# One unit's two 32-row inverse halves merged an iteration after their substitution, with a compact state worked in 64x64 tiles

## The chip, the cores and the metric

The kernel runs on one core of a Trainium2 chip. The metric is the device time of one execution in microseconds. TensorE is called PE here, VectorE DVE, ScalarE ACT, GpSimd POOL, and SyncE SP. All arithmetic is in 32-bit floats.

## The reference

A recurrence over 768 tokens (4 batches, 8 heads, head dimension 40), followed by a mixture of four small networks:

```python
for t in range(S):
    y[:, :, t] = np.einsum('bhd,bhde->bhe', rt, state)
    Sa = np.einsum('bhde,bhe->bhd', state, at)
    state = state * wt[:, :, None, :] - np.einsum('bhd,bhe->bhde', Sa, bt) \
          + np.einsum('bhd,bhe->bhde', vt, kt)
...
p = domain_probs / (domain_probs.sum(-1, keepdims=True) + 1e-09)
for e in range(E):                      # 4 networks, 320 -> 1024 -> 320
    h = np.maximum(x @ w1[e], 0.0)
    out += p[:, e:e + 1] * (h @ w2[e])
```

Here x is y with the heads side by side: 3072 tokens of 320 values.

## The kernel before

The tokens are cut into 12 chunks of 64. A *unit* is one chunk of two batches, so its 128 partitions hold 2 x 64 tokens; there are 24 units, numbered u = 0 to 23, two to a chunk (an even unit holds batches 0 and 1, an odd one batches 2 and 3). Inside a unit the recurrence is turned into matrix products, and these need the inverse of a unit triangular 64x64 matrix for each batch and head.

`within(u)` (L239) does what does not need the state. It transposes the decays (`pw`), forms their running product G with a scan (L247), transposes it back (`pg`), scales the inputs by G or 1/G (A, K, N; L256 to L264), transposes those (RT, VT, AT, NT, KT) and forms the products `pf`. DVE copies the 32x32 diagonal blocks of `pf` into `Fd` (L283, eight copies) and transposes them into X (L292). POOL then inverts all those blocks at once by substitution on X, with 60 dependent instructions (L296 and L300): **the substitution**. Beside it PE forms `pc`, `pyc`, `pe` and `pev`. Then comes **the merge**: DVE transposes X into QTc and Qc (L319, L320), POOL copies the diagonal blocks into QT (L331), PE forms `pY` and `pQ` from the 32-row halves (L336, L347), and ACT copies the off-diagonal block into QT (L352).

`step(u, xT)` (L358) does what needs the state, one link after another: `prh` from the state and AT, RH = prh + EV on DVE (L374), `prt` (RH transposed), `psa` from RHt and QT (the first use of the merged inverse), SaT, `pst`, `px`, the masked copy of `px` into TT on DVE (L236), the state's update (`psd` on PE, L411 and L412 on DVE), `py`, Y = py * G (L433), Y + YC on POOL (L434), and twelve small DMAs of Y into xT (L443).

`mixture(c)` (L449) runs the four networks on a finished chunk, in 32 *pieces* of PE work (`ph`, 6 matmuls, and `po`, 4 matmuls). The driver (L528) goes through the units: it writes step(u), then within(u + 2), and behind each `yield` one or two pieces of the mixture of the chunk before.

A scheduler fixes each engine's order when the kernel is built. It follows the order in which the code is written, but moves an instruction ahead where it counts the engine as free and the operands as ready. On the chip each engine runs its list in that order, and an instruction that waits holds up all that stand behind it on its engine. In the order before, POOL has: substitution u + 1, QT copies of u + 1, Y of u, substitution u + 2.

Of the kernel before, what the change touches and what calls it, by code (L numbers as in the profile page):

```python
# [15 lines left out]
def kernel(  # L16
# [12 lines left out]
):  # L29

# [90 lines left out]
    w_shift = kept("w_shift", [P, 2 * NJ, L], 1)  # L121
# [7 lines left out]
    state = [kept(f"state{i}_", [P, NJ, 2, 64], 1)() for i in range(B)]  # L129
# [7 lines left out]
    def load(u):  # L137
# [4 lines left out]
        for x in srcs:  # L142
            if x in nat:
                t = nat[x]()
            else:
                t = sb.tile([P, H, D], FP32, name=f"nat{x}", tag=f"nat{x}")
            q.n[x] = t
            for i, bb in enumerate(q.b):
                nc.sync.dma_start(
                    out=t[i * L:(i + 1) * L, :, 0:D],  # L150
                    in_=srcs[x][bb, :, q.c * L:(q.c + 1) * L, :].rearrange("h t e -> t h e"),
                )
# [41 lines left out]

    def heads(x):
        return x.rearrange("p (h e) -> p h e", e=64)
# [25 lines left out]
    def from_tokens(name, x, m):  # L222

        p = big(name)
        for j in range(NJ):
            for s in range(2):
                h = 2 * j + s
                nc.tensor.matmul(  # L228
                    out=p[half(s), j * P:(j + 1) * P], lhsT=x[:, h, :], rhs=m[:, h, :], start=True, stop=True,
# [3 lines left out]
    def causal(p):  # L233
        m = TT()
        for s in range(2):
            nc.vector.copy_predicated(out=of_slot(m[:], s), mask=over_heads(mask_up), data=p[s])  # L236
        return m

    def within(q):  # L239
# [7 lines left out]
        nc.vector.tensor_tensor_scan(  # L247
            out=q.G[:].rearrange("p c i -> p (c i)"), data0=ws[:].rearrange("p c i -> p (c i)"),
# [9 lines left out]
        nc.vector.tensor_tensor(out=A[:, :, 0:D], in0=pg, in1=n["A"][:], op=ALU.mult)  # L258
# [8 lines left out]
        def turned(name, x, keep=False):  # L267
            t = sb.tile([P, NJ, P], FP32, name=name, tag=name if keep else "turned", bufs=2)
            nc.scalar.copy(out=t[:].rearrange("p j t -> p (j t)"), in_=turn("p" + name, tok(x))[:])
            return t  # L270

        q.RT = turned("RT", n["R"], True)
        VT = turned("VT", q.V)
        yield 1
        q.AT = turned("AT", A, True)
        NT = turned("NT", q.N)
        yield 1
        pf = products("pf", q.AT, NT)
        F10 = sb.tile([P, H, Q], FP32, name="F10")
# [10 lines left out]
        X = sb.tile([P, Q, Q], FP32, name="X", tag="q", bufs=3)  # L290
# [11 lines left out]
        KT = turned("KT", q.K)  # L302
        pc = products("pc", VT, q.RT)
        CT = causal(pc)
        yield 1
        pyc = from_tokens("pyc", q.K, CT)
        q.YC = sb.tile([P, 2 * NJ, L], FP32, name="YC", tag="YC", bufs=2)
        nc.vector.tensor_tensor(out=q.YC[:], in0=heads(pyc[:]), in1=q.G[:], op=ALU.mult)
        pe_ = products("pe", KT, q.AT)
        ET = causal(pe_)  # L310
        yield 1
        pev = from_tokens("pev", q.V, ET)
# [4 lines left out]
        Qc = sb.tile([P, Q, Q], FP32, name="Qc", tag="q", bufs=3)  # L317
        QTc = sb.tile([P, Q, Q], FP32, name="QTc", tag="q", bufs=3)
# [38 lines left out]

    def step(q, xT):  # L358
# [4 lines left out]
        else:  # L363
            prh = big("prh")
            for j in range(NJ):
                for i in range(2):
                    for s in range(2):
                        o = j * P + i * L
                        nc.tensor.matmul(  # L369
                            out=prh[half(s), o:o + L], lhsT=state[q.b[i]][:, j, s, :],  # L370
                            rhs=q.AT[:, j, i * L:(i + 1) * L], start=True, stop=True,
# [3 lines left out]
            SN = sb.tile([P, 2, NJ, 2, 64], FP32, name="SN", tag="q", bufs=3)  # L375
            for i in range(2):
                st = state[q.b[i]]
                psn = turn("psn", lambda j: st[:, j].rearrange("p s d -> p (s d)"))
# [190 lines left out]
```

## Time and profile before

| | |
|---|---|
| median of 3 runs | 2204.19 us (2201.79 to 2204.97) |
| the profiled execution, time | 2210.9 us |
| the profiled execution, span | 2209.1 us |
| PE busy | 1522.0 us (69%) |
| POOL busy | 803.4 us (36%) |
| DVE busy | 636.7 us (29%) |
| ACT busy | 318.3 us (14%) |
| mean granted clock of PE | 0.833 |

The span is what the trace covers; the time holds 1.8 us more around it. In a row of the timeline the first number is the start and the second the time taken, both in microseconds from the span's start; then come the engine, the line of the kernel, the operation, output<-input, and how many instructions the row joins. Brackets give the idle time before the row and who ended it.

### The profile page before, as it was taken

Reading aid. Unit: us, or ns where it says so; the run is one execution under the profiler, and the core shown is the slowest. Engines: PE = TensorE matmul, PEld = TensorE weight load, DVE = VectorE, ACT = ScalarE, POOL = GpSimd, SP = SyncE. Lnnn points to the kernel's source line nnn. Section 1 sums busy time; section 2 is a strip of 40 time slices with the busy share of each in tenths; the row PEclk is TensorE's granted clock in tenths of the full one; section 3 lists DMA queues with packets and bytes.
Section 4 is the critical chain, followed back from the end, with each engine's and each line's share of the span. In section 5 each row is a group of like instructions: output and inputs, shape, how many; then the busy total and the mean of one; then the engine's idle time right before and its main releaser. Section 6 shows DMA issues by size and latency. Waiting matters only on the chain.

```text
span 2209.1 us, 28307 instructions
## 1 busy us (share of the span) xinstructions
PE 1522.0 (69%) x11592; PEld 1115.2 (50%) x11592; DVE 636.7 (29%) x930; ACT 318.3 (14%) x667; POOL 803.4 (36%) x1596
## 2 busy tenths in 40 slices
PE   2232765965955957858669587595596695875999
PEld 2222553653743745546447355374374463654766
DVE  2323341422413323223134043242331322323100
ACT  1100111111111111112112111111111111111110
POOL 2556335235145054152351432523505505325000
PEclk9656777977978979879788798797797887978999
DMA  8001110100101101011011011010010100100000
GB/s 229 16 3 19 22 20 2 28 8 16 26 6 19 23 7 22 7 22 23 4 25 23 1 28 20 3 29 5 18 25 7 19 13 16 22 2 9 8 7 7
DMA packets 179088, 44.62 MB, mean 20 GB/s; under 512 B 159504, under 2 KB 177936, under 8 KB 178960
## 3 DMA queue, kind: packets, MB, share of 16 engines
q1 hardware_dynamic: 168336, 32.28, 8.0%
q10 hardware_dynamic: 10624, 10.54, 1.5%
q8 instruction: 92, 1.51, 0.3%
q14 instruction: 36, 0.29, 0.0%
HBM read 34.13 MB, written 3.93 MB: 17 GB/s over the span
## 4 chain that ended last, share of the span: by engine, by line
PE 48%; POOL 34%; DVE 11%; issue 5%; DMA 1%; ACT 0%; SPq 0%; ACTq 0%; DVEq 0%; POOLq 0%
POOL X L300 17%; POOL tmp L296 16%; PE po L477 16%; PE ph L458 11%; DVE Fd L283 6%; PE ph L464 4%; DVE QTc L319 2%; PE psd L402 2%; PE prh L369 1%; PE psn L205 1%; DVE X L292 1%; PE px L216 1%; PE pf L216 1%; PE pQ L347 1%; PE psa L228 1%
## 5 line engine op out<-in xcount | busy, mean ns | idle before, releaser
L296 POOL TENSOR_TENSOR tmp<-X 128x30 f32<-128x30 f32 (+4 forms) x720 | 348.1, 483 | 545.4 <-DVE X L292 490.9
L477 PE MATMUL po<-w_sb,hs 128*128 128x320 f32 x1536 | 489.6, 468 | 0.0
L336 PE MATMUL pY<-QTc,F 32*32 32x32 f32 x768 | 25.5, 236 | 577.3 <-DVE QTc L319 577.3
L458 PE MATMUL ph<-xT,w_sb 128*128 128x256 f32 x1536 | 390.6, 395 | 2.9 <-DMA xT<-Y 2.9
L300 POOL TENSOR_TENSOR X<-X,tmp 128x30 f32<-128x30 f32 (+4 forms) x720 | 369.6, 513 | 56.4
L477 PEld LDWEIGHTS po<-w_sb,hs 128*128 128x128 f32 x1536 | 296.4, 202 | 119.4 <-issue 20.0
L336 PEld LDWEIGHTS pY<-QTc,F 32*32 32x32 f32 x768 | 23.0, 150 | 586.9 <-issue 568.6
L458 PEld LDWEIGHTS ph<-xT,w_sb 128*128 128x128 f32 x1536 | 277.6, 192 | 69.1 <-issue 29.3
L434 POOL TENSOR_TENSOR Y<-Y,YC 128x512 f32<-128x512 f32 x24 | 33.4, 1391 | 623.5 <-issue 538.9
L319 DVE STREAM_TRANSPOSE QTc<-X 128x1024 f32<-128x1024 f32 x24 | 47.6, 1983 | 686.4 <-POOL X L300 686.4
L283 DVE COPY_PREDICATED Fd<-mask_low,pf 32x128 f32<-32x128 int32 x192 | 139.0, 724 | 115.1 <-PE pf L216 112.4
L471 ACT ACTIVATE hs<-ph 128x512 f32<-128x512 f32 x192 | 104.3, 594 | 409.1 <-PE ph L464 408.8
L464 PE MATMUL ph<-xT,w_last 64*128 64x256 f32 x768 | 148.2, 436 | 0.0
L342 ACT COPY Yq<-pY 32x256 f32<-32x256 f32 x48 | 17.4, 362 | 649.7 <-PE pY L336 649.1
L236 DVE COPY_PREDICATED TT<-mask_up,px 128x512 f32<-128x512 int32 x48 | 32.1, 721 | 236.0 <-PE px L216 236.0
L464 PEld LDWEIGHTS ph<-xT,w_last 64*128 64x128 f32 x768 | 63.2, 188 | 69.1 <-issue 67.7
L487 DVE SCALAR_TENSOR_TENSOR osb<-po,gate,osb 128x320 f32<-128x320 f32 x72 | 39.3, 546 | 188.8 <-PE po L477 187.6
L228 PE MATMUL pyc<-TT,k_tok 128*64 128x128 f32 x384 | 39.3, 300 | 38.5 <-DVE TT L236 28.7
L331 POOL COPY QT<-QTc 32x256 f32<-32x256 f32 x96 | 37.9, 395 | 52.9 <-DVE QTc L319 49.9
L228 PEld LDWEIGHTS pyc<-TT,k_tok 128*64 128x64 f32 x384 | 27.6, 149 | 53.8 <-issue 23.0
L259 DVE RECIPROCAL gp<-gp 128x320 f32<-128x320 f32 x24 | 51.4, 2143 | 0.0
L247 DVE TENSOR_TENSOR_SCAN G<-w_shift,first 128x512 f32<-128x512 f32 x24 | 29.4, 1225 | 70.7 <-ACT w_shift L245 70.4
(108 smaller groups left out, 1569.4 us busy)
## 6 DMA issues: line engine op xcount, KB each, us to landing
w_sb<-in_moe_w_dram ACTq DMA_DIRECT2D x4, 1280.0 KB
w_sb<-in_moe_w_dram ACTq DMA_DIRECT2D x8, 512.0 KB
natK<-in_k_dram SPq DMA_DIRECT2D x48, 80.0 KB
natB<-in_b_dram SPq DMA_DIRECT2D x48, 80.0 KB
natA<-in_a_dram SPq DMA_DIRECT2D x48, 80.0 KB
natW<-in_w_dram SPq DMA_DIRECT2D x48, 80.0 KB
natV<-in_v_dram SPq DMA_DIRECT2D x48, 80.0 KB
natR<-in_r_dram SPq DMA_DIRECT2D x48, 80.0 KB
```

Source lines behind the costliest of these rows:

```text
L216: nc.tensor.matmul(out=p[s][:, j * P:(j + 1) * P], lhsT=lhsT[half(s), j, :], rhs=rhs[half(s), j, :], start=True, stop=True,)
L228: nc.tensor.matmul(out=p[half(s), j * P:(j + 1) * P], lhsT=x[:, h, :], rhs=m[:, h, :], start=True, stop=True,)
L259: nc.vector.reciprocal(out=gp[:], in_=gp[:])
L283: nc.vector.copy_predicated(out=fd[o, :, NJ * s:NJ * s + NJ].rearrange("p c j -> p j c"), mask=mask_low[o, None, :].to_broadcast([Q, NJ, Q ...
L296: nc.gpsimd.tensor_tensor(out=t, in0=X[:, j:j + 1, j + 1:Q].to_broadcast([P, j, m]), in1=X[:, 0:j, j:j + 1].to_broadcast([P, j, m]), op=AL ...
L300: nc.gpsimd.tensor_tensor(out=X[:, 0:j, j + 1:Q], in0=X[:, 0:j, j + 1:Q], in1=t, op=ALU.add)
L319: nc.vector.transpose(out=QTc[:].rearrange("p h r -> p r h"), in_=X[:].rearrange("p c r -> p r c"))
L336: nc.tensor.matmul(out=py[quarter(i - 1), hh * Q:(hh + 1) * Q], lhsT=F10[quarter(i), h, :], rhs=QTc[quarter(i), hh, :], start=True, stop=True,
L458: nc.tensor.matmul(out=ph[f % 2][:, f // 2, :], lhsT=w1_sb[:, e, g, (f0 + f) * P:(f0 + f + 1) * P], rhs=xT[:, g, :], start=(g == 0), stop= ...
L464: nc.tensor.matmul(out=ph[i][:, f // 2, :], lhsT=w1_last[i * DT:(i + 1) * DT, e, (f0 + f) // 2, :], rhs=xT[i * DT:(i + 1) * DT, 2, :], sta ...
L471: nc.scalar.activation(out=h[:], in_=ph[i][:], func=ACTF.Relu)
L477: nc.tensor.matmul(out=po[:], lhsT=hs[e, f // 4, f % 2][:, f % 4 // 2, s * P:(s + 1) * P], rhs=w2_sb[:, e, f, :], start=(f == 0), stop=(f ...
```

## The change

The merge leaves `within` and becomes a generator of its own, `merge(u)`. The driver now writes step(u), within(u + 2), merge(u + 1), so that the code of a merge stands one unit later than that of its substitution; X and F10 get two buffers for that, QTc and Qc share two instead of three with X.

The state loses the zero blocks that padded each pair of heads: 64 columns for a pair instead of 128. `prh` multiplies 64x64 tiles, one transpose instead of two gives the transposed state (`psn`, 4 matmuls instead of 8, one copy SN instead of two), and the state part of `py` multiplies 64x64 tiles in all four quadrants, into two PSUM tiles instead of one, so that Y = py * G is two DVE instructions. To let the heads meet, A, K and N are written in another head order, each by two DVE instructions of half the size, K now ahead of N; ACT negates the loaded B ahead of N (`nc.scalar.mul`), in place; the decays are loaded by eight DMAs instead of two; the masks and the output DMAs take the heads in the new order. The scan reads G itself, with a small POOL memset of its first column ahead of it, and `w_shift` is gone.

```diff
@@ load
-                nc.sync.dma_start(
-                    out=t[i * L:(i + 1) * L, :, 0:D],
-                    in_=srcs[x][bb, :, q.c * L:(q.c + 1) * L, :].rearrange("h t e -> t h e"),
-                )
+                to, src = t[i * L:(i + 1) * L, :, 0:D], srcs[x][bb, :, q.c * L:(q.c + 1) * L, :]
+                if x == "W":
+                    for h in range(4):
+                        nc.sync.dma_start(
+                            out=to[:, h // 2 + h % 2 * 2::4, :], in_=src[h::4].rearrange("h t e -> t h e"),
+                        )
+                else:
+                    nc.sync.dma_start(out=to, in_=src.rearrange("h t e -> t h e"))
@@ within
-        ws = w_shift()
-        nc.scalar.copy(out=ws[:, :, 1:L], in_=pwv[:, :, 0:L - 1])
         q.G = sb.tile([P, 2 * NJ, L], FP32, name="G", tag="G", bufs=2)
+        nc.gpsimd.memset(q.G[:, :, 0:1], 0.0)
+        nc.scalar.copy(out=q.G[:, :, 1:L], in_=pwv[:, :, 0:L - 1])
...
-        nc.vector.scalar_tensor_tensor(
-            out=q.N[:, :, 0:D], in0=n["B"][:], scalar=-1.0, in1=gp[:], op0=ALU.mult, op1=ALU.mult,
-        )
-        nc.vector.tensor_tensor(out=q.K[:, :, 0:D], in0=n["K"][:], in1=gp[:], op=ALU.mult)
+        nc.scalar.mul(out=n["B"][:], in_=n["B"][:], mul=-1.0)
+        to_e(q.K, lambda x, d, e: nc.vector.tensor_tensor(out=x, in0=d(n["K"]), in1=e(gp), op=ALU.mult))
+        to_e(q.N, lambda x, d, e: nc.vector.tensor_tensor(out=x, in0=d(n["B"]), in1=e(gp), op=ALU.mult))
...
-        F10 = sb.tile([P, H, Q], FP32, name="F10")
+        q.F10 = F10 = sb.tile([P, H, Q], FP32, name="F10", tag="F10", bufs=2)
...
-        X = sb.tile([P, Q, Q], FP32, name="X", tag="q", bufs=3)
+        q.X = X = sb.tile([P, Q, Q], FP32, name="X", tag="X", bufs=2)
...
         yield 1
-        Qc = sb.tile([P, Q, Q], FP32, name="Qc", tag="q", bufs=3)
-        QTc = sb.tile([P, Q, Q], FP32, name="QTc", tag="q", bufs=3)
+    def merge(q):
+        X, F10 = q.X, q.F10
+        Qc = sb.tile([P, Q, Q], FP32, name="Qc", tag="q", bufs=2)
+        QTc = sb.tile([P, Q, Q], FP32, name="QTc", tag="q", bufs=2)
         nc.vector.transpose(out=QTc[:].rearrange("p h r -> p r h"), in_=X[:].rearrange("p c r -> p r c"))
         nc.vector.transpose(out=Qc[:].rearrange("p h c -> p c h"), in_=X[:])
@@ step
-                            out=prh[half(s), o:o + L], lhsT=state[q.b[i]][:, j, s, :],
-                            rhs=q.AT[:, j, i * L:(i + 1) * L], start=True, stop=True,
+                            out=prh[half(s), o:o + L], lhsT=state[q.b[i]][half(s), j, :],
+                            rhs=q.AT[half(s), j, i * L:(i + 1) * L], start=True, stop=True,
...
+            for i in range(0 if start else 2):
+                for s, r in QUADS:
+                    o = jj * P + i * L
+                    nc.tensor.matmul(
+                        out=pys[r][half(s), o:o + L], lhsT=SN[half(r), i, jj, s, :],
+                        rhs=q.RT[half(r), 2 * jj + s, i * L:(i + 1) * L],
+                        start=False, stop=(i == 1),
+                    )
@@ driver
     drive(within(units[1]), 0, 1)
+    drive(merge(units[0]), 0, 1)
     for u in range(NU):
...
             gens.append(within(units[u + 2]))
+        if u + 1 < NU:
+            gens.append(merge(units[u + 1]))
         drive(chain(*gens), PIECES // 2, 14)
```

**PE, behind the substitution of unit 12.** pev closes within(12); F with a number is the off-diagonal block of one unit, and pY is the first product of a merge. Before, pY takes F_5637, which comes from pf of unit 12:

```order
L458 MATMUL ph<-xT,w_sb 128x256 x4
L464 MATMUL ph<-xT,w_last 128x256 x2
L228 MATMUL pev<-TT_112,natV_94 64x128 x8
L477 MATMUL po<-w_sb,hs 128x320 x9
L336 MATMUL pY<-QTc,F_5637 32x32 x16
```

In the changed kernel, at the same place on PE, pY takes F_5203, which comes from pf of unit 11:

```order
L505 MATMUL ph<-xT,w_sb 128x256 x4
L511 MATMUL ph<-xT,w_last 128x256 x2
L249 MATMUL pev<-TT_110,natV_94 64x128 x8
L524 MATMUL po<-w_sb,hs 128x320 x4
L375 MATMUL pY<-QTc,F_5203 32x32 x16
```

On PE the merge has moved: behind within(12) stands the merge of unit 11, whose substitution is an iteration old.

**DVE, at the substitution of an even unit.** Before, on DVE at unit 10: X_4649 is that unit's X; RH_4891 and px0_4964, px1_4965 belong to step(9).

```order
L319 STREAM_TRANSPOSE QTc_4799<-X_4649 128x32x32
L320 STREAM_TRANSPOSE Qc_4798<-X_4649 128x32x32
L487 SCALAR_TENSOR_TENSOR osb_4390<-po_4793,gate_149,osb_4390 128x320
L487 SCALAR_TENSOR_TENSOR osb_4391<-po_4850,gate_149,osb_4391 128x320
L374 TENSOR_TENSOR RH_4891<-prh_4874,EV_4288 128x512
L236 COPY_PREDICATED TT1_114<-mask_up_71,px0_4964 128x4x128
L236 COPY_PREDICATED TT1_114<-mask_up_71,px1_4965 128x4x128
```

The changed kernel, on DVE at unit 10 (X_4697 is its X; RH_4945 and px0_5012, px1_5013 are of step(9)):

```order
L358 STREAM_TRANSPOSE QTc_5352<-X_4697 128x32x32
L534 SCALAR_TENSOR_TENSOR osb_4431<-po_4841,gate_153,osb_4431 128x320
L359 STREAM_TRANSPOSE Qc_5351<-X_4697 128x32x32
L534 SCALAR_TENSOR_TENSOR osb_4432<-po_4898,gate_153,osb_4432 128x320
L415 TENSOR_TENSOR RH_4945<-prh_4928,EV_4329 128x512
L259 COPY_PREDICATED TT1_112<-mask_up_71,px0_5012 128x2x256
L259 COPY_PREDICATED TT1_112<-mask_up_71,px1_5013 128x2x256
```

On DVE the transposes of unit 10 have not moved: though written behind within(11), the scheduler puts them ahead of RH of step(9), as before, and only the copies osb stand otherwise.

**DVE, at the substitution of an odd unit.** Before, on DVE at unit 11 (X_5161; RH_5376 and px0_5450 are of step(10)):

```order
L487 SCALAR_TENSOR_TENSOR osb_4391<-po_5248,gate_149,osb_4391 128x320
L319 STREAM_TRANSPOSE QTc_5297<-X_5161 128x32x32
L320 STREAM_TRANSPOSE Qc_5296<-X_5161 128x32x32
L374 TENSOR_TENSOR RH_5376<-prh_5359,EV_4787 128x512
L236 COPY_PREDICATED TT0_112<-mask_up_71,px0_5450 128x4x128
```

The changed kernel, on DVE at unit 11 (X_5216; RH_5437 and px0_5505 are of step(10)):

```order
L534 SCALAR_TENSOR_TENSOR osb_4432<-po_5303,gate_153,osb_4432 128x320
L415 TENSOR_TENSOR RH_5437<-prh_5420,EV_4835 128x512
L358 STREAM_TRANSPOSE QTc_5862<-X_5216 128x32x32
L359 STREAM_TRANSPOSE Qc_5861<-X_5216 128x32x32
L259 COPY_PREDICATED TT0_110<-mask_up_71,px0_5505 128x2x256
```

Here RH of step(10) has come ahead of the transposes of unit 11; the copy of px still stands behind them. The two patterns alternate from unit 4 to unit 23. On POOL, from unit 3 on, the order is what it was (substitution, QT copies of the same unit, Y of the unit before), with the memset of the next G behind Y. On ACT the negation of B for the unit after next stands between the copies AT, NT and KT of a unit.

More of the change, by code (lines that the diff above doesn't have):

```diff
@@ L128 @@
     nc.vector.tensor_copy(out=fd[:], in_=diagf[:, :, None].to_broadcast([P, Q, Q]))
-    state = [kept(f"state{i}_", [P, NJ, 2, 64], 1)() for i in range(B)]
+    state = [kept(f"state{i}_", [P, NJ, 64], 1)() for i in range(B)]
     class Unit:
@@ L356, in within @@
         yield 1
+    QUADS = ((0, 0), (1, 1), (0, 1), (1, 0))
     def step(q, xT):
@@ L374, in step @@
             nc.vector.tensor_tensor(out=RH[:], in0=prh[:], in1=q.EV[:], op=ALU.add)
[L375 to L378, printed above, removed]
-                nc.scalar.copy(out=SN[:, i].rearrange("p j s d -> p (j s d)"), in_=psn[:])
+            SN = sb.tile([P, 2, 2, 2, 64], FP32, name="SN")
+            psn = turn("psn", lambda j: state[q.b[j // 2]][:, j % 2 * 2:j % 2 * 2 + 2, :].rearrange("p j d -> p (j d)"))
+            nc.scalar.copy(out=SN[:].rearrange("p i j s d -> p (i j s d)"), in_=psn[:])
         yield 1
@@ L382, in step @@
         nc.scalar.copy(
-            out=RHt[:].rearrange("p h e -> p (h e)"), in_=turn("prt", lambda j: RH[:, j * P:(j + 1) * P])[:],
+            out=RHt[:].rearrange("p h d -> p (h d)"), in_=turn("prt", lambda j: RH[:, j * P:(j + 1) * P])[:],
         )
         yield 1
-        psa = from_tokens("psa", RHt, q.QT)
+        psa = from_tokens("psa", d_head, lambda j, s: RHt[:, d_head(j, s), :], q.QT)
         SaT = sb.tile([P, NJ, P], FP32, name="SaT", tag="s", bufs=3)
@@ L394, in step @@
             )
-        XT = causal(products("px", SaT, q.RT))
+        XT = causal(products("px", SaT, q.RT), True)
         yield 1
@@ L408, in step @@
                 for s in range(2):
-                    x = state[q.b[i]][half(s), :, s, 0:D]
+                    x = state[q.b[i]][half(s), :, 0:D]
                     dx = pairs(pd[i][half(s), :])[:, :, s * 64:s * 64 + D]
```

101 lines of the change are left out of this document (60 added, 41 removed).

## The prediction, made before the changed kernel ran

> **What bounds the kernel now.** I read the page first, then the waits, then the timelines of DVE and PE over two units, then stretches of the clock. The page:
>
> ```profile
> span 2209.1 us, 28307 instructions
> PE 1522.0 (69%) x11592; PEld 1115.2 (50%) x11592; DVE 636.7 (29%) x930; ACT 318.3 (14%) x667; POOL 803.4 (36%) x1596
> ```
>
> No engine is full, so something goes round in a circle. The list of waits (total, times, longest):
>
> ```profile
> DVE QTc L319 <- POOL X L300: 686.4, 24, 30.2
> PE pY L336 <- DVE QTc L319: 577.3, 24, 31.1
> ```
>
> Each unit's merge waits for its substitution, and PE stands behind it for 24 us a unit. The DVE timeline of units 8 to 10 shows the circle:
>
> ```profile
> 715.66 1.97 DVE L319 STREAM_TRANSPOSE QTc<-X 128x1024 f32<-128x1024 f32 x1 [29.68 <-POOL X L300]
> 717.52 1.91 DVE L320 STREAM_TRANSPOSE Qc<-X 128x1024 f32<-128x1024 f32 x1
> 719.26 0.51 DVE L487 SCALAR_TENSOR_TENSOR osb<-po,gate,osb 128x320 f32<-128x320 f32 x1
> 729.56 0.69 DVE L374 TENSOR_TENSOR RH<-prh,EV 128x512 f32<-128x512 f32 x1 [0.54 <-PE prh L369]
> 773.76 1.25 DVE L292 STREAM_TRANSPOSE X<-Fd 128x1024 f32<-128x1024 f32 x1
> 809.67 1.99 DVE L319 STREAM_TRANSPOSE QTc<-X 128x1024 f32<-128x1024 f32 x1 [27.66 <-POOL X L300]
> 811.50 1.93 DVE L320 STREAM_TRANSPOSE Qc<-X 128x1024 f32<-128x1024 f32 x1
> 826.86 1.34 DVE L236 COPY_PREDICATED TT<-mask_up,px 128x512 f32<-128x512 int32 x2 [8.05 <-PE px L216]
> 831.20 0.68 DVE L411 TENSOR_TENSOR state<-psd,state 64x160 f32<-64x160 f32 x2 [3.00 <-PE psd L402]
> 833.31 0.67 DVE L412 TENSOR_TENSOR state<-state,gl 64x160 f32<-64x160 f32 x2
> 856.47 1.25 DVE L292 STREAM_TRANSPOSE X<-Fd 128x1024 f32<-128x1024 f32 x1
> 892.36 1.97 DVE L319 STREAM_TRANSPOSE QTc<-X 128x1024 f32<-128x1024 f32 x1 [29.67 <-POOL X L300]
> ```
>
> From X to the next QTc lie 35.9 us both times (773.76 to 809.67, 856.47 to 892.36): X itself, then 34.7 us of substitution. From QTc back to the next X lies PE's work. An interval that begins at an even unit's QTc (call it A) takes 809.67 - 715.66 = 94.01 us, one from an odd unit's (B) 892.36 - 809.67 = 82.69. PE in them:
>
> ```profile
> 717.77 1.06 PE L336 MATMUL pY<-QTc,F 32*32 32x32 f32 x32 [24.54 <-DVE QTc L319]
> 735.38 0.66 PE L205 MATMUL prt<-ident,RH 128*128 128x128 f32 x4
> 766.64 1.16 PE L216 MATMUL pf<-NT,AT 64*128 64x128 f32 x16
> 787.49 1.56 PE L458 MATMUL ph<-xT,w_sb 128*128 128x256 f32 x6
> 811.81 1.06 PE L336 MATMUL pY<-QTc,F 32*32 32x32 f32 x32 [22.76 <-DVE QTc L319]
> 833.65 0.44 PE L420 MATMUL py<-TT,n_tok 128*64 128x128 f32 x4
> 849.36 1.06 PE L216 MATMUL pf<-NT,AT 64*128 64x128 f32 x16
> 864.82 5.11 PE L477 MATMUL po<-w_sb,hs 128*128 128x320 f32 x18
> ```
>
> PE is dense from pY to pf and on to 789.05 (787.49 + 1.56) or 869.93, then stops until the next QTc.
>
> **What the change does to the circle.** The tables of order decide it. PE gets the merge one unit later and need not wait there. DVE does not: QTc of a unit still stands where it stood, right behind that unit's own work, and waits for the same substitution. In A the RH of the step stands behind QTc and Qc, so PE is let go at `prt`; in B only the copy of `px` stands behind them, and PE is let go at `py`. What PE used to do between QTc and these places goes under the substitution.
>
> A, after: QTc 1.97, osb 0.51, Qc 1.91, osb 0.51, RH 0.69 = 5.59; then `prt` to X as now, 773.76 - 735.38 = 38.38; then 35.91. Sum 79.88, a saving of 14.13. B, after: QTc 1.99, Qc 1.93, the copy of px 1.34 = 5.26; then `py` to X, 856.47 - 833.65 = 22.82; then 35.89. Sum 63.97, a saving of 18.72.
>
> Is PE in time? In A it has from one pf to the next `prt` 7.11 + 35.89 + 5.59 = 48.6 us and needs 20.57 (849.36 to 869.93) + 17.61 (717.77 to 735.38) = 38.2: 10 us idle at least. In B it has 7.12 + 35.91 + 5.26 = 48.3 and needs 22.41 (766.64 to 789.05) + 21.84 (811.81 to 833.65) = 44.2: 4 idle at least. A part of these needs ran at half clock and will not now, which adds about 4 and 3. So PE waits still, but for 14 and 7 us instead of 24.
>
> That brings the clock in. The stretches before and after pY of unit 9 (first number after the colon the length, then busy times; the clock is the third number from the end):
>
> ```profile
> 790.00:793.00 3.00, 0.00 (x0) 0.00 (x0) 0.00 (x0) 0.00 (x0) 2.61 (x6) 1.00 0.00 0
> 794.00:811.00 17.00, 0.00 (x0) 0.00 (x0) 1.33 (x1) 0.00 (x0) 13.52 (x28) 0.50 0.00 0
> 812.00:820.00 8.00, 8.00 (x110) 6.45 (x107) 2.12 (x2) 2.04 (x5) 1.31 (x4) 0.50 0.01 2
> 821.00:829.00 8.00, 8.00 (x60) 5.64 (x60) 1.34 (x2) 2.52 (x5) 0.00 (x0) 1.00 0.00 0
> ```
>
> The clock falls to 0.50 some 4 us after PE stops at 789.05, and comes back 8 to 9 us after it starts again. Before, those slow 8 us lay on pY, pQ and prh; now they lie on `prt` or `py` and what follows, on the path. Eight to nine us at half speed lose at most 4.3. I take 4 for A, where the wait is long, and 3 for B, where 7 us idle is nearer to the 4 us at which the clock falls. The bounds are 0 and 4.3. The Trainium skill ("TensorE: Matmul & The Clock Gate", Part 1) puts both the fall and the return at one window of about 3.4 us. The fall agrees with the rows; the return does not, and the rows decide.
>
> The other parts lie beside other work. The halved `psn` and the 64x64 `prh` are under the substitution now. The state part of `py` keeps its number of matmuls; at most its 16 could run wider, under 1 us, and I count nothing. K ahead of N and two DVE instructions for one put NT's source later by under 1 us; two mixture pieces stand between `pg` and `pAT`, which cover it. The second Y instruction and G's memset are on the way to the scan, where PE has a piece to do as well. If such covers fail, about 1 us a unit, 20 in all, and no row excludes the reverse sign. The negation of B and the DMAs of W come under the rivals.
>
> Ends of the run:
>
> ```profile
> 87.82 2.03 DVE L319 STREAM_TRANSPOSE QTc<-X 128x1024 f32<-128x1024 f32 x1 [30.02 <-POOL X L300]
> 165.81 1.23 DVE L247 TENSOR_TENSOR_SCAN G<-w_shift,first 128x512 f32<-128x512 f32 x1
> 217.31 1.99 DVE L319 STREAM_TRANSPOSE QTc<-X 128x1024 f32<-128x1024 f32 x1 [29.84 <-POOL X L300]
> 237.31 2.25 POOL L434 TENSOR_TENSOR Y<-Y,YC 128x512 f32<-128x512 f32 x1 [16.24 <-DVE Y L433]
> 291.39 1.98 DVE L319 STREAM_TRANSPOSE QTc<-X 128x1024 f32<-128x1024 f32 x1 [29.63 <-POOL X L300]
> 308.88 0.44 PE L420 MATMUL py<-TT,n_tok 128*64 128x128 f32 x4
> 365.77 1.99 DVE L319 STREAM_TRANSPOSE QTc<-X 128x1024 f32<-128x1024 f32 x1 [29.67 <-POOL X L300]
> 2039.79 1.98 DVE L319 STREAM_TRANSPOSE QTc<-X 128x1024 f32<-128x1024 f32 x1 [26.03 <-POOL X L300]
> 2057.99 0.44 PE L420 MATMUL py<-TT,n_tok 128*64 128x128 f32 x4
> ```
>
> Start: substitution 1 follows 0 on POOL at 87.82, with unit 0's four small QT copies among its steps, which I leave out: QTc of unit 1 at 87.82 + 34.7 = 122.5. On DVE stand then QTc 1.98, the state's update (two rows of 0.68, two of 0.67), Y (as large as RH, 0.69) and Qc 1.93 ahead of the scan of unit 2: 129.8. From that scan to QTc of unit 2 it took 217.31 - 165.81 = 51.5: 181.3. Y of unit 1 follows at once on POOL; from it to QTc of unit 3 291.39 - 237.31 = 54.1: 235.4. Then an interval like B: 5.26, from py 365.77 - 308.88 = 56.89, and 3 for the clock: QTc of unit 4 at 300.6 instead of 365.77, 65.2 saved.
>
> Middle: 19 intervals from 365.77 to 2039.79, 10 of A and 9 of B: 10 x (14.1 - 4) + 9 x (18.7 - 3) = 242.
>
> End: 2209.1 - 2039.79 = 169.3 now; after, 5.26, from py 2209.1 - 2057.99 = 151.1, the pY and pQ of unit 23 at 1.06 each, and 3: 161.5, so 7.8.
>
> Together 315. The profiled execution took 2210.9 (span plus 1.8): 1896. The median of the runs is 0.3% below that execution, 2204.19, so 1890. About 0.2% is what a measurement of this kernel can tell from no change.
>
> **Rivals.** *The cold starts cost little.* B's 7 us may not trip the clock, and the trace shows cold starts only with pY and pQ in front, whose 32x32 matmuls are hardly work. Without any loss 67 + 6 come off: 1823, in medians 1817. For it: the short wait in B. Against it: A's 14 us are three times those 4. By the skill's 3.4 us of return, 1.7 lost per start, an estimate would be 1855.
>
> *The negation of B holds ACT.* In each unit it waits on ACT for a DMA, with KT behind it. The order of SP's and ACT's work at unit 9:
>
> ```profile
> 763.55 1.41 SPq L149 DMA_DIRECT2D natW<-in_w_dram  x2
> 765.06 0.60 SPq L149 DMA_DIRECT2D natB<-in_b_dram  x1
> 774.37 0.59 ACT L269 COPY KT<-pKT 128x512 f32<-128x512 f32 x1
> ```
>
> W's eight issues take 5.6 instead of 1.4, and K's two now stand ahead, so B is issued at about 770.6 on this scale. If it lands within 4 us, KT waits for nothing. No row gives its landing; up to 11 us the 7 idle us of B take it. At 20 us PE would be late by 9 in each B, less the 3 of the clock, which then stays up: 9 x 6 = 54, so 1944.
>
> *Slower: the clock stays down.* If the waits keep PE at 0.50 through its whole dense part, that part doubles: `prt` to the end of pf, 32.4, in A, and `py` to the end of pf, 16.8, in B. Then 10 x 112.3 + 9 x 80.7 = 1849 instead of 1674; with some 50 saved at the start about 2336, in medians 2329. It turns into a loss from about 40 us lost per pair of units. Against it: in 821 to 829 the clock is at 1.00 under just this work.
>
> *The merge does not move.* If PE were held where it was, nothing changes: 2204. PE's order speaks against it.
>
> **Chances.** Forecast 0.60 (its own range 1855 to 1925), cheap cold starts 0.22, ACT held 0.13, no change 0.01, slower 0.04. 1815 to 1950 takes in the first three with the bounds of their unknowns. Faster 0.95, within 0.2% 0.01, slower 0.04.
>
> **What would show it.** In the profile after: PE's wait at pY gone, and waits at `prt` (for RH) and `py` (for TT) of some 14 and 7 us in turn; QTc still waiting for X on DVE; QTc to QTc about 84 and 67 us in turn; the clock at 0.50 at the start of both waits' ends; the first such interval from about 301. It is wrong if the intervals are alike, if PE waits elsewhere (KT, pc), or if POOL stands idle for longer than 50 us after an even unit.

## The result and the profile after

The changed kernel takes 1869.4 us in the median of 4 runs (1867.8 to 1871.2), beside 2204.0 us before on the same chip: ratio 0.848, 95% interval 0.847 to 0.850. The profiled execution is the run of 1869.15 us; its mean granted clock is 0.889 instead of 0.833. The prediction was 1890 (1815 to 1950). First the page:

```profile
span 1867.4 us, 28434 instructions
PE 1475.9 (79%) x11504; PEld 1078.4 (58%) x11504; DVE 641.2 (34%) x1026; ACT 318.0 (17%) x669; POOL 800.5 (43%) x1619
```

PE's busy time is 46 us less, at fewer matmuls and less time at half clock; POOL's is within 3 us of before. So 296 of the 342 us that the span lost came out of PE's idle time. The list of waits, to be held against the 686 and 577 us of before (total, times, longest):

```profile
DVE QTc L358 <- POOL X L337: 551.4, 24, 29.8
PE prt L220 <- DVE RH L415: 157.5, 10, 15.9
ACT natB L299 <- DMA natB<-in_b_dram: 102.6, 20, 9.2
PE py L461 <- DVE TT L259: 62.8, 14, 14.3
```

PE's wait at `pY` is gone. In its place stand ten waits at `prt` and the shorter ones at `py`, both behind DVE, which still waits for POOL. The DVE timeline has QTc of units 0, 1, 4 and 23, and between them one interval of each kind (units 10 to 12):

```profile
90.51 2.03 DVE L358 STREAM_TRANSPOSE QTc<-X 128x1024 f32<-128x1024 f32 x1 [9.76 <-POOL X L337]
126.60 1.98 DVE L358 STREAM_TRANSPOSE QTc<-X 128x1024 f32<-128x1024 f32 x1 [17.83 <-POOL X L337]
...
306.46 1.96 DVE L358 STREAM_TRANSPOSE QTc<-X 128x1024 f32<-128x1024 f32 x1 [29.82 <-POOL X L337]
...
746.82 2.01 DVE L358 STREAM_TRANSPOSE QTc<-X 128x1024 f32<-128x1024 f32 x1 [29.82 <-POOL X L337]
792.37 1.25 DVE L329 STREAM_TRANSPOSE X<-Fd 128x1024 f32<-128x1024 f32 x1
828.24 2.06 DVE L358 STREAM_TRANSPOSE QTc<-X 128x1024 f32<-128x1024 f32 x1 [17.96 <-POOL X L337]
831.95 1.31 DVE L259 COPY_PREDICATED TT<-mask_up,px 128x512 f32<-128x512 int32 x2
857.90 1.25 DVE L329 STREAM_TRANSPOSE X<-Fd 128x1024 f32<-128x1024 f32 x1
893.72 2.00 DVE L358 STREAM_TRANSPOSE QTc<-X 128x1024 f32<-128x1024 f32 x1 [29.82 <-POOL X L337]
...
1708.93 1.97 DVE L358 STREAM_TRANSPOSE QTc<-X 128x1024 f32<-128x1024 f32 x1 [23.26 <-POOL X L337]
```

A is 828.24 - 746.82 = 81.42 us, B is 893.72 - 828.24 = 65.48. PE in the same stretch:

```profile
752.02 1.12 PE L220 MATMUL prt<-ident,RH 128*128 128x128 f32 x4 [15.78 <-DVE RH L415]
...
794.11 2.07 PE L231 MATMUL pc<-RT,VT 64*128 64x128 f32 x14 [4.49 <-ACT F L325]
832.70 1.31 PE L461 MATMUL py<-TT,n_tok 128*64 128x128 f32 x8 [3.42 <-DVE TT L259]
```

It waits 15.8 us at `prt` and 3.4 at `py`, and also 4.5 at `pc`, which the prediction did not have. The clock behind the two wakes (length of the stretch, PE busy, clock):

```profile
752.00:756.00 4.00, 3.98 (x12) 0.50 0.00 0
833.00:838.00 5.00, 5.00 (x51) 0.50 0.00 0
```

PE still wakes at half clock, but full clock is back at 756.07 and 837.99 (rows further down), 4.1 us after the wake at `prt` and 5.3 after the one at `py`, where before the change it took 8 to 9 behind `pY` in the unit that the prediction read, and 7.2 to 10.7 over units 4 to 17. The Trainium skill ("TensorE: Matmul & The Clock Gate", Part 1) lets it return after one busy window of about 3.4 us; the rows are nearer to that than to the row I had priced it by.

The terms of the sum, in us of the profiled executions:

| term | predicted | measured |
|---|---|---|
| QTc of unit 4 | 300.6 | 306.46 |
| 19 intervals from there | 1674.0 - 242 = 1432 (the intervals named, 10 x 83.9 + 9 x 67.0, make 1442) | 1708.93 - 306.46 = 1402.5 |
| from QTc of unit 23 to the end | 161.5 | 1867.4 - 1708.93 = 158.5 |
| the profiled execution | 1896 | 1869.15 |

### The profile page after: what moved, and what is told of

Same layout as the page of the kernel before. It is cut to its first block, busy times and chain, and to the rows that moved or that the text cites. A ratio compares the mean times of both kernels' runs of the same rounds, so it can differ in the third digit from the quotient of the medians.

```text
span 1867.4 us, 28434 instructions
## 1 busy us (share of the span) xinstructions
PE 1475.9 (79%) x11504; PEld 1078.4 (58%) x11504; DVE 641.2 (34%) x1026; ACT 318.0 (17%) x669; POOL 800.5 (43%) x1619
## 4 chain that ended last, share of the span: by engine, by line
POOL 39%; PE 37%; DVE 13%; issue 8%; DMA 2%; SPq 1%; ACT 0%; ACTq 0%; DVEq 0%; POOLq 0%
POOL X L337 20%; POOL tmp L333 19%; PE po L524 15%; PE ph L505 8%; DVE Fd L320 7%; PE ph L511 3%; DVE Qc L359 2%; PE py L461 2%; DVE X L329 2%; PE pf L231 1%; PE py L468 1%; PE psd L441 1%; PE pg L220 1%; PE px L231 1%; PE prt L220 1%
## 5 line engine op out<-in xcount | busy, mean ns | idle before, releaser
L524 PE MATMUL po<-w_sb,hs 128*128 128x320 f32 x1536 | 475.9, 460 | 0.0
L505 PEld LDWEIGHTS ph<-xT,w_sb 128*128 128x128 f32 x1536 | 288.3, 198 | 59.9 <-issue 19.3
L220 PE MATMUL prt<-ident,RH 128*128 128x128 f32 x88 | 19.0, 353 | 157.5 <-DVE RH L415 157.5
L511 PE MATMUL ph<-xT,w_last 64*128 64x256 f32 x768 | 135.6, 428 | 0.2 <-DMA xT<-Y 0.2
L220 PEld LDWEIGHTS prt<-ident,RH 128*128 128x128 f32 x88 | 12.3, 175 | 165.3 <-DVE RH L415 161.5
L461 PE MATMUL py<-TT,n_tok 128*64 128x128 f32 x384 | 40.8, 338 | 62.8 <-DVE TT L259 62.8
L231 PE MATMUL pc<-RT,VT 64*128 64x128 f32 x384 | 49.7, 346 | 41.1 <-ACT F L325 36.3
L231 PEld LDWEIGHTS pc<-RT,VT 64*128 64x128 f32 x384 | 40.3, 236 | 49.4 <-ACT F L325 44.9
L461 PEld LDWEIGHTS py<-TT,n_tok 128*64 128x64 f32 x384 | 23.8, 161 | 77.3 <-DVE TT L259 70.4
L274 ACT COPY G<-pw 128x504 f32<-128x504 f32 x24 | 13.9, 578 | 265.8 <-PE pw L220 230.8
```

What stands on the lines that cost most here:

```text
L220: nc.tensor.transpose(out=p[:, j * P:(j + 1) * P], in_=src(j), identity=ident[:])
L231: nc.tensor.matmul(out=p[s][:, j * P:(j + 1) * P], lhsT=lhsT[half(s), j, :], rhs=rhs[half(s), j, :], start=True, stop=True,)
L461: nc.tensor.matmul(out=pys[r][half(s), jj * P:(jj + 1) * P], lhsT=q.N[:, h, :], rhs=XT[:, h, :], start=True, stop=start,)
L505: nc.tensor.matmul(out=ph[f % 2][:, f // 2, :], lhsT=w1_sb[:, e, g, (f0 + f) * P:(f0 + f + 1) * P], rhs=xT[:, g, :], start=(g == 0), stop= ...
L511: nc.tensor.matmul(out=ph[i][:, f // 2, :], lhsT=w1_last[i * DT:(i + 1) * DT, e, (f0 + f) // 2, :], rhs=xT[i * DT:(i + 1) * DT, 2, :], sta ...
L524: nc.tensor.matmul(out=po[:], lhsT=hs[e, f // 4, f % 2][:, f % 4 // 2, s * P:(s + 1) * P], rhs=w2_sb[:, e, f, :], start=(f == 0), stop=(f ...
```

## Experiments

All times are medians, and each ratio is to the kernel before, measured beside it on the same chip (2205 to 2206 us).

| kernel | us | ratio, 95% interval |
|---|---|---|
| merge put back | 2197.2 | 0.996 (0.994 to 0.997) |
| RH ahead of QTc | 1698.4 | 0.770 (0.769 to 0.771) |
| QTc behind the next ET | 1644.9 | 0.746 (0.745 to 0.747) |
| the same, QT copies on ACT | 1649.4 | 0.748 (0.747 to 0.749) |
| dummies, tile of the mixture | 1971.3 | 0.894 (0.893 to 0.895) |
| dummies, tile of prt and py | 1867.2 | 0.847 (0.846 to 0.848) |
| 64 small dummies | 1878.4 | 0.852 (0.851 to 0.853) |
| 240 small dummies | 1979.8 | 0.898 (0.897 to 0.899) |
| 8 wide dummies | 1902.6 | 0.863 (0.862 to 0.864) |
| natB negated on DVE | 1885.9 | 0.855 (0.854 to 0.856) |
| natB behind KT | 1869.8 | 0.848 (0.847 to 0.850) |
| QTc behind the next ET, natB behind KT | 1655.9 | 0.751 (0.749 to 0.752) |

### Is it the merge, or the compact state?

```diff
     drive(within(units[0]), 0, 1)
+    drive(merge(units[0]), 0, 1)
     load(1)
     drive(within(units[1]), 0, 1)
-    drive(merge(units[0]), 0, 1)
+    drive(merge(units[1]), 0, 1)
...
             gens.append(within(units[u + 2]))
-        if u + 1 < NU:
-            gens.append(merge(units[u + 1]))
+            gens.append(merge(units[u + 2]))
```

> The changed kernel with its compact state and 64x64 tiles kept, but each unit's merge put back right behind its own substitution, as before. Theory (the time comes from PE being let go by RH and px ahead of the substitution's end, and the compact state is worth nothing on the path): PE waits again at the merge's own matmuls, the unit intervals return to about 94 and 83 us, and the time is 2204 us within 20. Rival (the 64x64 tiles and the compact state save time on the path themselves): the time is well below 2204, and by as much as they are worth the 335 us measured for the whole change are not the merge's; with a third of it, 2090 us.

It took 2197.2 us. The waits of this kernel:

```profile
PE pY L375 <- DVE QTc L358: 533.1, 24, 31.1
```

PE stands at `pY` again, 533 us instead of 577. The compact state, the 64x64 tiles and the eight DMAs of W are worth 0.4% in that order, so the gain is the merge's place. That all these parts "lie beside other work" holds there. No run moves the merge without them, but two stretches of the path, in the experiment on the clock below, show that they are worth nothing there in the new order either.

### Is A long because of RH's place on DVE?

`issue_after(i)` keeps what an engine is given inside it behind instruction i in that engine's order; `mark` holds the RH of the step written before.

```diff
+        with (tc.issue_after(mark[0].ins) if mark else ExitStack()):
             nc.vector.transpose(out=QTc[:].rearrange("p h r -> p r h"), in_=X[:].rearrange("p c r -> p r c"))
             nc.vector.transpose(out=Qc[:].rearrange("p h c -> p c h"), in_=X[:])
...
-            nc.vector.tensor_tensor(out=RH[:], in0=prh[:], in1=q.EV[:], op=ALU.add)
+            mark[:] = [nc.vector.tensor_tensor(out=RH[:], in0=prh[:], in1=q.EV[:], op=ALU.add)]
```

> The changed kernel with one order on DVE changed: the two transposes QTc and Qc of a unit are issued behind the RH of the step that runs beside them, instead of ahead of it. Nothing else is changed. Theory (in the intervals of 81.4 us PE is held at prt because RH stands behind the transposes, which wait for POOL; in those of 65.5 us only px stands behind them): the two kinds of interval become alike at about 65.5 us, ten of them lose 16 us each, and the time is about 1710 us, 1690 to 1740; PE's wait at prt is gone and all its waits are at py. Rival (the long intervals are long because of their own work, the even unit's loads or its step, not because of RH's place): they stay at 80 us or more, and the time stays within 30 us of 1869.

It took 1698.4 us. Two units on DVE in this kernel:

```profile
692.30 2.10 DVE L361 STREAM_TRANSPOSE QTc<-X 128x1024 f32<-128x1024 f32 x1 [15.38 <-POOL X L337]
756.69 2.05 DVE L361 STREAM_TRANSPOSE QTc<-X 128x1024 f32<-128x1024 f32 x1 [17.64 <-POOL X L337]
805.67 0.69 DVE L418 TENSOR_TENSOR RH<-prh,EV 128x512 f32<-128x512 f32 x1 [0.54 <-PE prh L413]
821.75 2.10 DVE L361 STREAM_TRANSPOSE QTc<-X 128x1024 f32<-128x1024 f32 x1 [15.38 <-POOL X L337]
```

The rows are QTc of units 10, 11 and 12. RH now starts 16 us ahead of the even unit's QTc, behind which it stood. A takes 756.69 - 692.30 = 64.39 us and B 821.75 - 756.69 = 65.06, and the wait at `prt` is gone from the list. Ten intervals of A are 17 us shorter each, and 1698 is where the theory put it: the length of A is set by what the scheduler left behind QTc on DVE.

### What if DVE does not stand waiting at all?

The same device, with `mark` set to the copy of `pe` (ET, whose last instruction is `last`) in the next unit's `within`.

```diff
+        mark[:] = [last[0]]
         yield 1
...
+        with (tc.issue_after(mark[0].ins) if mark else ExitStack()):
             nc.vector.transpose(out=QTc[:].rearrange("p h r -> p r h"), in_=X[:].rearrange("p c r -> p r c"))
             nc.vector.transpose(out=Qc[:].rearrange("p h c -> p c h"), in_=X[:])
```

> The changed kernel with the transposes QTc and Qc issued on DVE behind the next unit's ET, so that the merge truly starts a unit after its substitution and DVE does not stand waiting for POOL. The four copies of the diagonal blocks into QT stay on POOL, where they now stand behind the next unit's substitution. Theory (POOL runs in order: substitution of 34.7 us, then the copies 1.7 us, then the step's work from psa to Y's add on PE and ACT and the next within up to pf, about 29 us, then F and X 7 us): one unit takes about 73 us whatever its parity, and the time is 1850 us, 1800 to 1920: the wait moves from DVE to PE waiting for QT at psa, and nothing is won over the changed kernel. Rival (DVE standing behind QTc is all that holds PE): with it gone PE becomes the bound at about 60 us a unit, and the time is near 1600 us.

It took 1644.9 us, so the theory fell and the rival was nearer. The theory's premise was wrong. POOL in this kernel:

```profile
781.27 0.68 POOL L339 TENSOR_TENSOR X<-X,tmp 128x228 f32<-128x228 f32 x1
781.89 0.39 POOL L374 COPY QT<-QTc 32x256 f32<-32x256 f32 x1
782.24 0.58 POOL L335 TENSOR_TENSOR tmp<-X 128x220 f32<-128x220 f32 x1
```

The scheduler put the four copies among the next substitution's steps, 24 us after its X began (757.78), and not behind it. X to X on DVE in this kernel:

```profile
757.78 1.25 DVE L331 STREAM_TRANSPOSE X<-Fd 128x1024 f32<-128x1024 f32 x1
821.34 1.25 DVE L331 STREAM_TRANSPOSE X<-Fd 128x1024 f32<-128x1024 f32 x1
882.04 1.25 DVE L331 STREAM_TRANSPOSE X<-Fd 128x1024 f32<-128x1024 f32 x1
```

Ten units of it in one stretch (length, then busy time of PE, PEld, DVE, ACT and POOL, and PE's clock):

```profile
634.00:1255.00 621.00, 583.83 (x4878) 427.88 (x4877) 270.98 (x430) 131.82 (x280) 326.91 (x660) 0.98 0.12 23
```

Units take 63.6 and 60.7 us in turn, and PE is busy for 94% of the stretch. PE is the bound here. This is the fastest version, 12% below the changed kernel by their medians.

With the copies on ACT as well (`nc.scalar.copy` for `nc.gpsimd.tensor_copy`):

> The kernel with the transposes behind the next unit's ET, and the four copies of the diagonal blocks into QT on ACT instead of POOL. Theory (the merge then waits for no engine that has a substitution ahead of it): PE waits neither at prt nor at py, and a unit is set by PE's own work, about 60 to 62 us, the chain of substitution, Y's add, G, scan, pg, pf and X taking about 56 us beside it: 1550 to 1630 us, and PE's clock stays at 1.00 in the middle. Rival (POOL's chain of substitution and what stands between two of them sets a unit in any order): about 73 us a unit and 1850 us, as with the copies on POOL.

It took 1649.4 us, no faster: the intervals are 63.6 to 65.0 and 60.1 to 61.8 in turn, but for the last. The theory's range ended 1% too low, and its reason for preferring ACT was the same wrong premise.

### Are the 1.5 us an interval the clock's?

A measured 81.42 against 79.88 of instructions in the sum, B 65.48 against 63.97. Dummies in PE's wait should keep the clock up:

```diff
+    def spin(n):
+        t = ps.tile([P, DM], FP32, name="spin", tag="mm", bufs=4)
+        for _ in range(n):
+            nc.tensor.matmul(out=t[:], lhsT=ident[:], rhs=w2_sb[:, 0, 0, :], start=True, stop=True)
...
+        if q.bp == 1 and q.u > 2 and q.u < NU - 2:
+            spin(23)
...
+        if q.bp == 0 and q.u > 2 and q.u < NU - 2:
+            spin(3)
```

> The changed kernel with dummy 128x320 products added on PE where it stands waiting, whose results nobody reads: 23 ahead of prt in odd units, 3 ahead of py in even units, in the middle of the run (units 3 to 21). Nothing of the work changes. Theory (each interval pays about 1.5 us because PE's clock is 0.50 when it wakes: 81.4 against 79.9 of instructions at full clock, 65.5 against 64.0): with the clock kept at 1.00 each of about 19 intervals is 1.5 us shorter, and the time is 1842 us, 1835 to 1850. Rival (the 1.5 us are not the clock's, but waits that the sum left out): the time stays within 5 us of 1869, or grows where a dummy outlasts the wait.

It took 1971.3 us and says nothing on the question. PE's list of waits in this kernel shows why:

```profile
PE spin L402 <- DVE osb L543: 130.3, 10, 13.1
```

The dummies' tile belonged to the mixture's pool, and its buffer came free through an `osb` that stands behind QTc on DVE. So they ran after the wait, not in it. In the second try `spin` is given the tile that `prt` or `py` overwrites afterwards:

```diff
+        prt = big("prt")
+        if q.bp == 1 and q.u > 2 and q.u < NU - 2:
+            spin(prt, 23)
...
         pys = [big(f"py{r}") for r in range(2)]
+        if q.bp == 0 and q.u > 2 and q.u < NU - 2:
+            spin(pys[0], 3)
```

> The dummies once more, as in the run before this one that meant to keep PE's clock up (23 ahead of prt in odd units, 3 ahead of py in even ones, results overwritten), but written into the PSUM tile of prt and of py themselves, which are free when PE stops, so that they run inside the wait: 46 passes of 0.29 us are 13.3 us of the 15.8 at prt, 6 are 1.7 us of the 3.4 at py. Theory (each interval pays about 1.5 us because the clock is 0.50 at the wake): the clock shows 1.00 at prt and py, the intervals fall from 81.4 and 65.5 to about 80 and 64, and the time is 1842 us, 1832 to 1852. Rival (the 1.5 us are waits that the sum left out): 1869 us within 6.

It took 1867.2 us. PE in it, in an interval of A and in two of B:

```profile
737.59 12.65 PE L401 MATMUL prt<-w_sb,ident 128*128 128x320 f32 x46
753.34 0.66 PE L220 MATMUL prt<-ident,RH 128*128 128x128 f32 x4 [3.10 <-DVE RH L419]
832.05 1.88 PE L401 MATMUL py<-w_sb,ident 128*128 128x320 f32 x6 [3.29 <-DVE TT L259]
833.86 0.66 PE L470 MATMUL py<-TT,n_tok 128*64 128x128 f32 x8
...
1269.24 3.57 PE L401 MATMUL py<-w_sb,ident 128*128 128x320 f32 x6 [3.89 <-DVE TT L259]
```

The X that follows each of the first two places, on DVE:

```profile
791.71 1.25 DVE L329 STREAM_TRANSPOSE X<-Fd 128x1024 f32<-128x1024 f32 x1
856.63 1.25 DVE L329 STREAM_TRANSPOSE X<-Fd 128x1024 f32<-128x1024 f32 x1
```

The clock behind the wake at `prt`, and at the `py` of 833.86:

```profile
753.50:759.00 5.50, 5.50 (x40) 1.00 0.00 0
834.50:835.00 0.50, 0.50 (x20) 1.00 0.00 0
```

At `prt` the dummies lay in the wait. In eight of the ten long intervals the clock stayed at 1.00, and these take 79.5 to 79.6 us, against 81.4 in the changed kernel and 79.88 in the sum. From `prt` to X it is 791.71 - 753.34 = 38.37 us, the 38.38 of before the change; the changed kernel takes 792.37 - 752.02 = 40.35. In the other two the clock fell in the 3.3 us between the dummies' end and `prt`, and they took 81.2. For A the theory holds: 1.9 us are the clock's.

At `py` the dummies waited for TT themselves and ran behind the wake. In seven of the nine short intervals they ran at half clock (3.57 us in the row of 1269.24) and these grew from 65.5 to about 67.2, so the time did not move. In the other two the clock had stayed up. There `py` to X takes 856.63 - 833.86 = 22.77 us, the 22.82 of before, against 857.90 - 832.70 = 25.20 in the changed kernel. So the cold start costs 2.4 us in B. B is only 1.5 us over the sum because PE was let go earlier than summed: `py` starts 832.70 - 828.24 = 4.46 us after QTc, not 5.26, ahead of the end of the two copies of px (831.95 + 1.31), and in A `prt` starts 5.20 us after QTc, not 5.59.

That these two stretches take what they took before, at full clock, shows too that the compact state and the 64x64 tiles neither gain nor cost anything there.

### What brings the clock back early or late?

`small` makes 64, or 240, products of two 32x32 slices of RH; `wide` in its place makes 8 of two 128x128 slices.

```diff
+        if q.bp == 1 and q.u > 2 and q.u < NU - 2:
+            small(RH)
         RHt = sb.tile([P, H, 64], FP32, name="RHt", tag="s", bufs=3)
```

> The changed kernel with 64 dummy 32x32 products, whose results nobody reads, added on PE ahead of prt in odd units, released by the same RH as prt (ten units); 32 such took 1.06 us at clock 0.50. The question is why the clock came back 8.7 to 10.4 us after PE's wake before, where pY and pQ led, and 4.0 us after it here, where prt led. Theory (small products at the head hold the clock's return back): it comes back 7 us or more after the wake, and the ten long intervals grow from 81.4 to about 84 or 85 us: 1869 plus 25 to 35, about 1900 us. Rival (what leads does not matter, it is the length of the idle time or chance): the return stays at about 4 us, and the intervals grow by what the dummies take, 1 to 2 us: 1880 to 1888 us, like the run with wide dummies.

> The control: the changed kernel with 8 dummy 128x128 products in place of the 64 small ones, at the same place, released by the same RH; 4 such took 1.12 us at clock 0.50, so that both kinds of dummies last about 2.2 us there. Both theories: the clock comes back about 4 us after the wake, and the ten long intervals grow by 1 to 2 us: 1880 to 1888 us. What the small ones cost more than these is the clock's.

> The changed kernel with 240 dummy 32x32 products ahead of prt in odd units instead of 64, which last 7.2 us at clock 0.50 if they run at it throughout (64 took 1.93), so that whole steps of the 3.41-us grid on which the clock changed in the runs so far hold nothing else. Theory (small products count like any others): the clock comes back 3.4 to 6.8 us after the wake, while the dummies are still running, and they last about 5 to 6 us. Rival (small products do not wake the clock, which would explain the late return before the change): it comes back only after the dummies' end and one more step, 9 us or more after the wake, and they last 7.2 us. The time itself grows in both cases, by 35 to 90 us.

They took 1878.4, 1902.6 and 1979.8 us. With 64 small products ahead the clock came back 3.3 to 5.1 us after the wake, no later than with `prt` in front, and A grew to 82 or 83 us. The theory that small products hold it back falls. With the 8 wide ones it came back 4.2 to 5.1 after; they took 3.78 us, not the 2.2 that I had taken from transposes, and the time was 15 us above what was expected. 240 small ones, in stretches of 3.41 us between the points at which the clock can change (length, PE busy, clock; x counts records, two to a product):

```profile
624.84:628.25 3.41, 3.21 (x238) 0.50 0.02 5
628.25:631.66 3.41, 1.29 (x128) 1.00 0.02 5
```

PE in the same place:

```profile
624.63 3.42 PE L403 MATMUL small<-RH 32*32 32x32 f32 x238 [15.21 <-DVE RH L421]
...
633.57 1.81 PE L403 MATMUL small<-RH 32*32 32x32 f32 x114 [2.71 <-issue]
```

A stretch that holds nothing but small products brings the clock up; one that is 38% full (1.29 of 3.41) lets it fall again. In other units the gaps of 1.0 to 2.7 us "issue" between the bursts fell so that no stretch was full before the dummies' end (53 to 69% in four in a row at 781.84 to 795.50), and the clock came back 14 to 17.6 us after the wake. So each expectation of the clock met one part of the units, while the dummies lasted 10 to 12.7 us, which neither had; the size of the products is not what decides.

That the changes lie on a grid is to be seen in the changed kernel itself, in half microseconds (the mean clock says where in the half it changed):

```profile
756.00:756.50 0.50, 0.50 (x4) 0.93 0.00 0
793.50:794.00 0.50, 0.00 (x0) 0.62 0.64 114
800.00:800.50 0.50, 0.50 (x2) 0.55 0.00 0
831.00:831.50 0.50, 0.00 (x0) 0.67 0.00 0
837.50:838.00 0.50, 0.50 (x2) 0.51 0.00 0
```

Up at 756.07, down at 793.62, up at 800.45, down at 831.17, up at 837.99: the distances are 11, 2, 9 and 2 times 3.413 us (81.92 us are 24 steps). Call these points marks, and what lies between two of them a step. The wake at 752.02 met a mark at 752.66 and had its full step by 756.07; the wake at 832.70 lost the rest of its step to the mark at 834.58 and had to fill the next. That is 4.05 and 5.29 us. The Trainium skill ("TensorE: Matmul & The Clock Gate", Part 1) has a free-running window of that length, and here the trace agrees. Before the change the return came after two or three steps that the records show as busy, with `pY`, `pQ` and `prh` in them. With the wide dummies a step filled with `py` at half clock (845.22 to 848.64 in that run) did not bring the clock up either. What those steps lacked isn't settled.

### Is ACT's wait for natB on the path?

First the negation moved to DVE (`nc.vector.tensor_scalar_mul` behind K for `nc.scalar.mul` ahead of it):

> The changed kernel with the negation of natB moved from ACT to DVE, behind the product that makes k_tok, so that ACT does not stand waiting for natB's DMA (102.6 us over 20 units) with the copies of F queued behind it. Theory (ACT's wait lies beside PE's slack of 14 to 16 us an interval, so that nobody on the path waits for it): PE's wait at pc is gone, its wait at prt or py grows by as much, and the time is 1869 us within 8, slower rather than faster by what the 0.5 us instruction on DVE adds ahead of n_tok. Rival (the wait is on the path, the price of the rival on record, through F10 and pc): the time falls by 20 us or more.

It took 1885.9 us, 16 more, twice what was allowed for. DVE in this kernel:

```profile
867.23 0.33 DVE L300 TENSOR_SCALAR natB<-natB 128x320 f32<-128x320 f32 x1 [1.18 <-DMA natB<-in_b_dram]
867.47 1.24 DVE L329 STREAM_TRANSPOSE X<-Fd 128x1024 f32<-128x1024 f32 x1
```

The scheduler put the negation for the unit to come right ahead of X, the last link to POOL. There its 0.33 us and the 1.18 us of waiting for natB's DMA are on the path, so this run added a wait and says little about the one on ACT. So once more, left on ACT, but behind the copy of KT that `copied` holds, the one written last:

```diff
+        with (tc.issue_after(copied[0].ins) if copied else ExitStack()):
             nc.scalar.mul(out=n["B"][:], in_=n["B"][:], mul=-1.0)
```

> The changed kernel with the negation of natB (for the next unit) left on ACT but put behind the copy of KT, so that the copies of F and KT no longer stand behind natB's DMA, and nothing is added to DVE. Theory (ACT's wait and PE's wait at pc behind it lie inside slack that PE waits out at prt and py anyway): PE's wait at pc (36 us in all) is gone, its waits at prt and py grow by as much, and the time is 1869 us within 10. Rival (the price on record for ACT held by the negation, here through F and pc): faster by 20 us or more.

It took 1869.8 us, the changed kernel's time. PE in it:

```profile
790.01 1.16 PE L231 MATMUL pc<-RT,VT 64*128 64x128 f32 x14 [0.43 <-ACT F L330]
832.53 1.30 PE L466 MATMUL py<-TT,n_tok 128*64 128x128 f32 x8 [8.60 <-DVE TT L259]
```

The wait at `pc` is gone, and the wait at `py` has grown from 3.4 to 8.6 us. ACT's wait lay in slack. Then the same edit in the fastest version, where PE is the bound:

> The kernel with the transposes QTc and Qc behind the next unit's ET (1645 us, intervals of 63.6 and 60.7 us in turn), with the negation of natB put behind the copy of KT as well. There PE is the bound, so that what was slack in the changed kernel is not: theory: PE's wait at pc of 4 to 5 us in every second unit and the cold start behind it go, the intervals of 63.6 us fall to 58 to 60, and the time is 1600 us, 1585 to 1620. Rival (ACT's wait only moves, to EV or KT's successors, and PE waits there instead): 1645 us within 10.

It took 1655.9 us, 11 more instead of 45 less. The PE timeline there:

```profile
725.09 1.98 PE L249 MATMUL psa<-QT,RHt 128*64 128x128 f32 x16 [5.54 <-POOL QT L379]
```

PE now stands at `psa` for the QT copies, which POOL has among the next substitution's steps: 5.5 us in every second unit, with a cold start behind it. The wait moved, as the rival had it (its 1645 within 10 missed by one), but to a place that neither named.

## Why the prediction was right, point by point

**The circle and who lets PE go.** Right, and shown: the waits stand at `prt` for RH and at `py` for TT in turn, undoing the merge's place brings back 2197 us, and taking RH from behind QTc makes A as short as B.

**A and B at full clock, 79.88 and 63.97.** A is confirmed by the run with the clock held up, 79.5. In B the term behind the wake, `py` to X, is confirmed (22.77 for 22.82). The terms 5.59 and 5.26 were 0.4 and 0.8 us too long: durations were added up that overlap.

**The clock, 4 and 3 us.** The mis-sized term. A full return of 8 to 9 us was priced, from `pY` in front; it came in 4.1 and 5.3, and cost 1.9 us in A and 2.4 in B. The bounds 0 to 4.3 held it. With PE let go earlier than summed, each interval came out about 1.5 us over its sum instead of 4 and 3. So the middle gains 10 x 2.5 + 9 x 1.5 = 39 us over the 242 predicted.

**The single interval of before.** 10 x 94.01 + 9 x 82.69 = 1684.3, but the 19 intervals take 1674.0: the pair of intervals read was 10 us too long for the sum. Before the change, from unit 8 on, two kinds of pairs come in turn, of about 94.0 and 82.7 us and of 92.7 and 82.0, and the pair read is of the longer kind. So 242 + 39 - 10 = 271, and measured is 1674.0 - 1402.5 = 271.5.

**The start, 65.2 saved.** 59.3 came (365.77 - 306.46). The first QTc came at 90.51 instead of 87.82, which had been taken over from before, and unit 1's followed 36.1 us later instead of 34.7, with the four copies that were left out. These make 4.1 of the 5.9 missing; 1.8 are in the three steps after.

**The end, 7.8 saved.** 10.8 came (169.3 - 158.5). The forecast of the profiled execution was 27 us too slow in all, and it would have been 43 without the two errors the other way, at the start (6) and from the pair read (10): in part that is luck.

**PE's idle time, 14 and 7 us.** 15.8 and 3.4, and 4.5 at `pc`. A wait at `pc` was named as a sign of error. It came from the negation of B, whose DMA held ACT for 102.6 us over 20 units, with copies of F behind it. That is the mechanism of the rival, but not its price: as its own bound had it, what fits into B's idle time costs nothing, and moving it changed nothing. The 54 us did not come.

**The other parts at nothing.** Right within 0.4% in the order of before, and within 0.1 us on `prt` to X and `py` to X in the new one. **The clock staying down**: it came up at every wake.

## What to carry to other kernels

A merge moved later in the code is only as late as the scheduler leaves it: read on each engine what stands behind the instruction that waits, since that alone decides what is let go, and here two instructions' order was worth 171 us beyond the change. Take a mean interval for a sum, not a single one. A wait is worth only what the next one leaves: when the one at `pc` was taken away, PE stood longer at `py`, and in the fastest version at `psa`. A cure that adds an instruction ahead of the last link costs at once.

## What the hardware showed that was not expected

- The clock changed only at marks 3.413 us apart, so what a cold start costs depends on where the wake falls. With the 8 wide dummies in odd units alone, A grew by 2.2 us and B, which had none, by 1.1: the return behind `py` came 7.4 us after the wake instead of 5.3.
- A and B together came out at a whole number of such steps in several kernels: 146.9 us (43.0 steps) in the changed one, 150.2 (44.0) with the wide dummies, 146.7 (43.0) with the dummies in the tiles of prt and py. That the wake's place on the grid pulls them there is argued, not shown; the versions with intervals near 65 or 62 us mostly do not show it (129.5 and 124.3 us, 37.9 and 36.4 steps).
- Of the 240 small products in a row (480 records) the first 171 to 256 records ran in one burst, and the rest in bursts of up to 128 with gaps of 1.0 to 2.7 us before each, so that they took up to 12.7 us for 7.3 us of work.
